# Scheduler priority for a recurrent chain, earlier K and Q copies, and a wider, doubled staging buffer

## The chip, the cores and the metric

The kernel runs on one core of a Trainium2 chip. The metric is the time on the device in microseconds. Executions of one kernel agree within about 1% here, so ratios are given with a 95% interval. A ratio is the mean time of one kernel's fast runs over that of the other's fast runs of the same rounds, so it is not quite the ratio of the medians that are quoted beside it.

## The reference, cut to what matters

```python
for s in range(n_seg):                      # 64 segments of 32 tokens
    h = concatenate([mem, x[:, 32*s:32*s+32]])   # 8 memory rows + 32 tokens, 448 wide
    q, k, v = h @ Wq, h @ Wk, h @ Wv        # 16 heads of 256
    p = softmax(mask(q k^T * scale))
    o = (p v) @ Wo
    mem = o[:, :8]                          # the next segment needs it
    outs.append(o[:, 8:])
h  = x + concatenate(outs)                  # x goes in after a layer norm
h2 = h + (silu(n(h) @ w_gate) * (n(h) @ w_up)) @ w_down
# the result, and the gradients of x, mem0 and all seven weights
```

The memory rows make 64 steps that cannot overlap, once forward and once backward.

## The kernel before

After each segment the kernel keeps K and Q, transposed as TensorE made them, and turns them token by token again for the backward stage. That side work ("spill") runs per tile of four segments, called r0 to r3 after their place in it. K's four jobs are done in r3, Q's four in the next r0; the eight memory rows of a segment are spilled likewise after each sixteenth.

```python
def _tm_quarter(stg, dst_rows, q, nrows, eng):        # one spill job
    pt = ps1(BF16)
    for j in range(8):
        c = q * 8 + j
        nc.tensor.transpose(pt[:, j * P:(j + 1) * P], stg[:, c, :], ident[:, :])
    for hq in range(2):
        tmq = work.tile([P, 512], BF16, name="tmq", bufs=1)
        k.evac(tmq[:], pt[:, hq * 512:(hq + 1) * 512], eng)   # ScalarE for K, VectorE for Q
        nc.sync.dma_start(out=dst_rows[:, ...], in_=tmq[0:nrows, :])
# per segment s, r = s % 4
ps_v = wpass(Wv_sb, s)  # ... vT, then qT and kT
# scores -> pS;  transposes of vT -> V_sb
run_deferred(4)                                        # Q's jobs (r0)
with tc.high_priority(offset=4000):
    # softmax, P_sb, transposes of P -> PT_sb
nc.vector.tensor_copy(out=qT_x[:, :, r * SEG:(r + 1) * SEG], in_=qT[:, :, 0:SEG])
nc.scalar.copy(out=kT_x[:, :, r * SEG:(r + 1) * SEG], in_=kT[:, :, 0:SEG])
if r == 3:
    tok_major_x(kT_x, ...)                             # queue K's jobs
    run_deferred(4)                                    # and do them here
# P times V -> oT, times Wo -> memory rows (VectorE) and outputs (ScalarE)
# r == 3: tok_major_x(qT_x, ...)                       # queue Q's jobs
# ... [cut: sixteenths]
```

`evac` copies a result out of the accumulators. A scheduler orders each engine's instructions from priorities and from a model of durations, so the program's order is not the built order.

## Time and profile before

5248.1 us median of 4 runs. The stages, from the trace (the end of a segment is the copy of its memory rows):

| stage | us |
|---|---|
| up to the end of the first segment | 90.9 |
| 62 further forward segments (mean 27.4) and the last | 1699.1 + 25.3 |
| drain: from there to the first feed-forward product | 103.6 |
| feed-forward, backward weights | 553.1 + 74.5 |
| first backward segment, 63 further ones (mean 25.0) | 30.2 + 1573.3 |
| weight gradients (tail) | 1089.4 |

In profile lines PE is TensorE (PEld its weight loads), ACT is ScalarE, DVE is VectorE, POOL is GpSimd and SP is SyncE; psh and psf are accumulator tiles. A line of "A <- B: total, times, longest" in the list of waits names the engine that waited and the instruction it waited for. In the view in order of time a line has start, duration, engine, line of the kernel, what was written from what, and in brackets the idle time ahead of it and who ended it. The lines themselves stand in the prediction.

### The profile page before, as it was taken

To read this page: it belongs to the slowest core of one execution; us is meant where nothing else is said; L and a number is where in the kernel's file an instruction comes from. 1 tells how busy PE (TensorE), PEld (TensorE's weight loads), DVE (VectorE), ACT (ScalarE), POOL (GpSimd) and SP (SyncE) were. 2 spreads that over 40 slices of the span, in tenths; PEclk is the share of its full clock that TensorE was granted. 3 is DMA by queue.
4 is the path that set the end of the run, shared out by engine and by line. 5 is a ranking of instruction groups with operands and counts; after the bars stand their busy time and mean duration, and the time that the engine had idled before them with its cause. 6 is when DMAs were issued, how large, how long until landed. Compare 5 with 4: busy or idle time off the path is not lost.

```text
span 5239.3 us, 201704 instructions
## 1 busy us (share of the span) xinstructions
PE 4092.1 (78%) x94192; PEld 3447.6 (66%) x94192; DVE 2149.7 (41%) x4166; ACT 1581.2 (30%) x2722; POOL 396.2 (8%) x809
## 2 busy tenths in 40 slices
PE   4777777777777737776688888888888798987849
PEld 3777777777777624333688888888888755544525
DVE  3444444444444335554333333333333344645520
ACT  2222222332232233332323222232222344342420
POOL 2000000000000100000101011011000100000100
PEclk8888888888888868898798888888888799998879
DMA  4111211111111211112523233233223333333452
GB/s 160 49 50 57 67 48 48 62 59 57 54 56 46 86 64 61 62 59 71 163 88 94 86 99 91 86 92 100 86 86 88 121 103 122 112 120 103 140 181 92
DMA packets 221334, 454.17 MB, mean 87 GB/s; under 512 B 47072, under 2 KB 126080, under 8 KB 212624
## 3 DMA queue, kind: packets, MB, share of 16 engines
q1 hardware_dynamic: 180160, 284.12, 16.9%
q0 software_dynamic: 40336, 157.14, 9.2%
q8 instruction: 737, 12.08, 1.0%
q14 instruction: 101, 0.83, 0.1%
HBM read 228.30 MB, written 208.12 MB: 83 GB/s over the span
## 4 chain that ended last, share of the span: by engine, by line
PE 48%; ACT 7%; DMA 7%; DVE 6%; issue 3%; SPq 0%; ACTq 0%; POOL 0%; DVEq 0%; POOLq 0%
PE psf L790 15%; PE psf L933 8%; ACT dO_sb L59 4%; PE psf L717 3%; PE psf L980 2%; PE psf L1014 2%; PE psf L662 2%; PE psh L894 1%; PE psf L593 1%; DMA Kx<-tmq 1%; PE psf L348 1%; PE psf L769 1%; PE psf L778 1%; PE psf L728 1%; DMA out_dram<-wres 1%
## 5 line engine op out<-in xcount | busy, mean ns | idle before, releaser
L933 PE MATMUL psf<-ktg,H_all 128*128 128x512 bf16 x1920 | 420.1, 381 | 6.6 <-ACT acc L59 6.6
L933 PEld LDWEIGHTS <-H_all 128*128 128x128 bf16 x1920 | 187.8, 98 | 233.5 <-issue 11.7
L796 DVE CAST doutT_all<-psf 128x24 bf16<-128x24 f32 x63 | 11.5, 183 | 775.5 <-PE psf L790 775.5
L790 PE MATMUL psf<-dvT,WvT_sb 128*128 128x40 bf16 x8192 | 298.0, 191 | 25.3 <-issue 24.8
L790 PE MATMUL psf<-dkT,WkT_sb 128*128 128x40 bf16 x8192 | 289.7, 189 | 15.8 <-issue 15.6
L790 PE MATMUL psf<-dqT,WqT_sb 128*128 128x40 bf16 x8192 | 283.8, 188 | 13.2 <-issue 13.1
L790 PEld LDWEIGHTS <-WvT_sb 128*128 128x128 bf16 x8192 | 271.1, 108 | 32.9 <-issue 27.4
L493 PE MATMUL psf<-oT,Wo_sb 128*128 128x40 bf16 x8192 | 271.2, 198 | 11.0 <-DVE oT L57 5.3
L790 PEld LDWEIGHTS <-WkT_sb 128*128 128x128 bf16 x8192 | 266.8, 106 | 18.2 <-issue 17.7
L493 PEld LDWEIGHTS <-Wo_sb 128*128 128x128 bf16 x8192 | 269.8, 109 | 12.8 <-issue 6.3
L790 PEld LDWEIGHTS <-WqT_sb 128*128 128x128 bf16 x8192 | 261.1, 105 | 14.8 <-issue 14.6
L59 ACT COPY dO_sb<-psh 40x1024 bf16<-40x1024 bf16 x256 | 238.4, 1006 | 100.5 <-PE psh L748 100.5
L803 ACT COPY dxnT_tile<-psf 128x96 f32<-128x96 f32 x64 | 15.2, 238 | 809.5 <-DVE doutT_all L797 797.9
L348 PE MATMUL psf<-hT_roll,Wk_sb 128*128 128x40 bf16 x8192 | 224.4, 179 | 26.2 <-issue 25.6
L894 PE MATMUL psh<-ident,kstg 128*128 128x128 bf16 x2048 | 156.7, 250 | 106.6 <-DVE kstg L886 106.6
L446 PE MATMUL psh<-ident,P_sb 40*40 40x40 bf16 x1024 | 42.5, 191 | 249.2 <-DVE P_sb L442 249.2
L348 PEld LDWEIGHTS <-Wk_sb 128*128 128x128 bf16 x8192 | 213.2, 96 | 32.1 <-issue 31.7
L940 DVE TENSOR_TENSOR acc<-acc,psf 128x512 f32<-128x512 f32 x288 | 194.8, 687 | 89.4 <-PE psf L933 88.3
L348 PE MATMUL psf<-hT_roll,Wv_sb 128*128 128x40 bf16 x8192 | 218.5, 181 | 13.9 <-DVE hT_roll L498 13.9
L348 PEld LDWEIGHTS <-Wv_sb 128*128 128x128 bf16 x8192 | 217.5, 97 | 18.1 <-issue 18.1
L717 PE MATMUL psf<-doutT_all,WoT_sb 128*128 128x40 bf16 x8192 | 218.6, 180 | 13.7 <-DVE doutT_all L796 9.0
L717 PEld LDWEIGHTS <-WoT_sb 128*128 128x128 bf16 x8192 | 217.3, 96 | 14.6 <-issue 12.6
(290 smaller groups left out, 7350.4 us busy)
## 6 DMA issues: line engine op xcount, KB each, us to landing
VT_all<-vT SPq DMA_DIRECT2D x64, 320.0 KB, 2.6
OT_all<-oT POOLq DMA_DIRECT2D x64, 320.0 KB, 2.8
vT_b<-VT_all SPq DMA_DIRECT2D x64, 320.0 KB, 3.3
dVT_all<-dvT SPq DMA_DIRECT2D x64, 320.0 KB, 2.6
dKT_all<-dkT POOLq DMA_DIRECT2D x64, 320.0 KB, 4.1
dQT_all<-dqT SPq DMA_DIRECT2D x64, 320.0 KB, 4.6
Kx<-tmq SPq DMA_DIRECT2D x128, 128.0 KB, 2.3
Qx<-tmq SPq DMA_DIRECT2D x128, 128.0 KB, 2.0
```

The lines of the kernel that those rows point to most:

```text
L59: nc.scalar.copy(out=out, in_=in_)
L348: nc.tensor.matmul(o, lhsT=W_sb[:, kc, c * P:(c + 1) * P], rhs=hT_roll[:, kc, sl, :], start=(kc == 0), stop=(kc == KC - 1))
L493: nc.tensor.matmul(pO[:, mc * L:(mc + 1) * L], lhsT=Wo_sb[:, c, mc * P:(mc + 1) * P], rhs=oT[:, c, :], start=(c == 0), stop=(c == MC - 1))
L593: nc.tensor.matmul(pg[:, 0:f1 - f0], lhsT=hnT[:, kc, :], rhs=Wg_sb[:, kc, f0:f1], start=(kc == 0), stop=(kc == KC - 1))
L662: nc.tensor.matmul(pdh[:, 0:D], lhsT=srcT[:, c, :], rhs=WT[:, c, :], start=(i == 0), stop=(i == nmm - 1))
L717: nc.tensor.matmul(o, lhsT=WoT_sb[:, kc, c * P:(c + 1) * P], rhs=doutT_all[:, kc, s, :], start=(kc == 0), stop=(kc == KC - 1))
L790: nc.tensor.matmul(pH[0:msz, mc * L:(mc + 1) * L], lhsT=WT[:, c, mcols], rhs=dT[:, c, :], start=(i == 0), stop=(i == 3 * MC - 1))
L894: nc.tensor.transpose(pt[:, j * P:(j + 1) * P], stg[:, c, :], ident[:, :])
L933: nc.tensor.matmul(pacc[:, :], lhsT=H_all[:, kt, mc * P:(mc + 1) * P], rhs=KT_sb[:, sl, ncn * 512:(ncn + 1) * 512], start=(i == 0), stop=( ...
L940: nc.vector.tensor_tensor(out=dst, in0=dst, in1=pacc[:, :], op=ALU.add)
L980: nc.tensor.matmul(pacc[:, 0:D], lhsT=KT_sb[:, sl, mc * P:(mc + 1) * P], rhs=dOut_all[:, kt, :], start=(i == 0), stop=(i == len(slots) - 1))
L1014: nc.tensor.matmul(pacc[:, 0:f1 - f0], lhsT=HN_all[:, kt, mc * P:(mc + 1) * P], rhs=X_all[:, kt, f0:f1], start=(kt == 0), stop=(kt == NT - 1))
```

## The change

Its intent is to keep the chain of dependent work ahead of everything else. The chain gets the highest priority in program order (`crit`), forward and backward; K and Q are copied out right after their projections, and the spill jobs are queued before the softmax; the spill gets a wider, doubled buffer. To make room, the input window shrinks from 12 slots to 8, qT and kT to one buffer.

```diff
+    def crit(self):                       # class _Prio; next starts at -50_000_000
+            off = self.tc.cur_priority - self.next
+            with self.tc.high_priority(offset=off):
+                yield
+                self.next = self.tc.cur_priority
-        NWIN = 12
+        NWIN = 8
-        for hq in range(2):
-            tmq = work.tile([P, 512], BF16, name="tmq", bufs=1)
-            k.evac(tmq[:], pt[:, hq * 512:(hq + 1) * 512], eng)
-            nc.sync.dma_start(out=dst_rows[:, q * 1024 + hq * 512:q * 1024 + (hq + 1) * 512], in_=tmq[0:nrows, :])
+        tmq = work.tile([P, 1024], BF16, name="tmq", bufs=2)
+        k.evac(tmq[:], pt[:, 0:1024], eng)
+        nc.sync.dma_start(out=dst_rows[:, q * 1024:(q + 1) * 1024], in_=tmq[0:nrows, :])
-    prep_tile(1)
-    prep_load(2)
+    prep_load(1)
-            prep_tile(t + 2)
+            prep_tile(t + 1)
...
+        with k.prio.crit():               # projections; likewise softmax, P times V, Wo
+            if r == 0:
+                nc.vector.tensor_copy(out=qtmp[:], in_=qT[:, :, 0:SEG])   # parked for r1
...
+            nc.scalar.copy(out=kT_x[:, :, r * SEG:(r + 1) * SEG], in_=kT[:, :, 0:SEG])
...
+        if r == 3:
+            tok_major_x(kT_x, dr["Kx"][t * P:(t + 1) * P, :], P, "s")
+            tok_major_x(qT_x, dr["Qx"][t * P:(t + 1) * P, :], P, "v")
         run_deferred(4)
-        with tc.high_priority(offset=4000):
+        with k.prio.crit():               # softmax
-        if r == 3:
-            tok_major_x(kT_x, dr["Kx"][t * P:(t + 1) * P, :], P, "s")
-            run_deferred(4)
...                                         # backward: two crit blocks round the same chain
```

## The prediction

> **What bounds the kernel now.** I first read the page's busy shares, which cover three stages with different limits: a forward recurrence of 64 segments (0 to 1815 us), a feed-forward stage, a backward recurrence of 64 segments (2550 to 4150 us) and weight gradients. The diff touches the two recurrences and the drain behind the first. Each segment needs the last one's memory rows, so a recurrence costs the sum of its segments' latencies. Next the list of who waited for whom:
>
> ```profile
> POOL P_all L449 <- DVE P_sb L442: 1328.5, 63, 26.2
> ...
> PE psh L446 <- DVE P_sb L442: 249.2, 64, 6.7
> ...
> ACT tmq L59 <- DMA Kx<-tmq: 230.3, 105, 14.8
> ...
> DVE tmq L57 <- DMA Qx<-tmq: 131.8, 71, 3.2
> ...
> POOL hn_t L580 <- DMA Km<-tmq: 85.5, 1, 85.5
> ```
>
> GpSimd's long waits cost nothing: it only issues stores. TensorE's 249 us is the softmax, 3.9 us in each of 64 segments. ScalarE and VectorE, which must also serve the chain, stand for 360 us in front of tmq, the one staging buffer through which transposed K and Q leave for memory: each copy waits until the previous store has landed. The last line is one wait of 85 us. I then read the order-of-time view of two neighbouring segments:
>
> ```profile
> 824.34 3.14 PE L358 MATMUL psh<-ident,kT_x 128*128 128x128 bf16 x32
> ...
> 827.41 1.18 PE L484 MATMUL psf<-PT_sb,V_sb 40*128 40x40 bf16 x32
> ...
> 847.78 0.59 ACT L59 COPY tmq<-psh 128x512 bf16<-128x512 bf16 x1 [3.47 <-DMA Kx<-tmq]
> 848.26 1.05 ACT L455 COPY kT_x<-kT 128x1024 bf16<-128x1024 bf16 x1
> ...
> 849.51 1.91 ACT L59 COPY V_sb<-psh 40x1024 bf16<-40x1024 bf16 x2
> 850.71 0.42 DVE L57 COPY tmq<-psh 128x512 bf16<-128x512 bf16 x1 [2.47 <-ACT V_sb L59]
> 851.32 0.74 ACT L436 ACTIVATE S_sb<-S_sb 40x640 f32<-40x640 f32 x1
> ```
>
> The reader sees the K transposes stand between the P transposes and P times V, and in the next segment a spill copy that waits for a store push the V copies and the exponential back by about 3 us. From the same view I took phase means, leaving out the first tile; segments are named by place in a tile of four (r0 to r3). r2, where no spill runs, is the clean one:
> - whole segment: r0 28.7, r1 27.8, r2 24.5, r3 27.6 us; the three after each sixteenth, with the extra memory-row spills, 28.3, 28.4, 29.3.
> - scores to exponential: 7.3, 7.0, 4.4, 4.8; P transposes to P times V: 1.2, 1.3, 1.2, 4.0; waiting for the first projection: 0.9, then 0.05.
>
> So the excess over r2 (4.2, 3.3, 0, 3.1) is all of the kind that the change addresses. Behind the last segment:
>
> ```profile
> 1815.00:1938.00 123.00, 38.08 (x332) 27.80 (x329) 34.82 (x113) 37.71 (x66) 11.56 (x78) 0.60 0.30 93
> ```
> ```profile
> 1832.99 0.58 ACT L59 COPY tmq<-psh 128x512 bf16<-128x512 bf16 x1 [14.85 <-DMA Kx<-tmq]
> ...
> 1907.75 0.58 ACT L59 COPY tmq<-psh 128x512 bf16<-128x512 bf16 x1 [1.98 <-DMA Km<-tmq]
> ...
> 1910.56 0.16 POOL L580 MEMSET hn_t<- 128x64 bf16 x1 [85.48 <-DMA Km<-tmq]
> ```
>
> From 1815 to 1938 us every compute engine is idle two thirds of the time. The feed-forward buffers lie where the forward pools were, so they wait for the last of some 28 staged stores, 2.45 us each, after a first stall of 15 us behind the weight loads.
>
> The backward recurrence is different: TensorE is busy 88% there, its orders are nearly final, and only the first segment of each tile is longer (26.05 us against 24.2 to 24.9).
>
> [...] at 847.78 the ready V copies stand 3.47 us behind a copy that waits for a store. [...] 128 KB stores land in 2.0 to 2.3 us, 256 KB ones (gradient results) in 2.4. So one store of twice the size costs little more than one of the small.
>
> **The change part by part.** I compared the built order of the changed kernel with the old one.
>
> 1. Staging: 128x1024 copies instead of pairs of 128x512, in two buffers instead of one. A copy costs 1.0 us on ScalarE and 0.7 on VectorE (the 40x1024 and 128x1024 copies of this trace) against 2 x 0.58 and 2 x 0.42. Per job the chain copy, store, copy, store of about 5 us becomes half of 1.0 + 2.4: about 1.6 us. So four jobs fit into one segment and no longer spill into the next.
>
> 2. Order: the chain has its own top priority, and Q and K are copied out right after their projections. In the new order the K transposes (r3) stand before the P transposes, under the softmax; three of four input transposes move there in r0. The clean r2 keeps its order except for trivial swaps: 24.5 stays.
> - r1: no staging is left in it: 27.8 becomes 24.6, saving 3.2.
> - r3: P transposes to P times V falls by 2.75, but one ScalarE copy of 1.0 us now stands before the exponential (+0.7 against its old 4.8) and two later ones wait for a store, delaying the attention output by perhaps 0.2: 25.8, saving 1.8.
> - r0: input transposes save 0.3 before the first projection; the exponential comes at 4.9, not 7.3 (an input copy of 0.59 stands before it); VectorE has two Q copies and the move of the parked first quarter of Q (0.43) inside the softmax, +0.3; output copies +0.3: 26.4, saving 2.3.
> - after a sixteenth: 26.4, 25.0, 26.1, saving 1.9, 3.4, 3.2.
> Sum: 12 x 2.3 + 12 x 3.2 + 15 x 1.8 + 3 x (1.9 + 3.4 + 3.2) = 27.6 + 38.4 + 27 + 25.5 = 118 us.
>
> 3. Drain: K leaves within the last segment; 12 wide jobs stay. Two stores queue behind the weight loads (17 us, as now), then 10 jobs at 1.7 us, plus some waiting for the transposed feed-forward weights that the new order mixes in, about 7: the buffers are free 41 us after the chain instead of 95. I take 52 off, as weight transposes may hold the first tile.
>
> 4. Backward: the layer-norm work (3.9 us of VectorE, an input copy) moves from the head of a tile, where doT waits for it, to the time under the long last product:
> ```profile
> 2750.17 0.66 PE L811 MATMUL psf<-identf,dxnT_tile 128*128 128x128 f32 x4 [0.66 <-ACT dxnT_tile L803]
> ...
> 2755.54 0.37 PE L728 MATMUL psf<-vT_b,doT 128*40 128x40 bf16 x8 [0.52 <-DVE doT L57]
> ```
> Three of the four transposes go too. Of the excess of about 1.4 us I take 1.1, 15 times: 16 us.
>
> 5. Start: one input tile is prepared before the first projection, not three: 3 us. The smaller window (8 slots) and the single qT and kT buffers are free of waits, as their readers finish within the segment.
>
> Total 118 + 52 + 16 + 3 = 189; 5248 - 189 = 5059, say 5060 us, 3.6% less.
>
> **The rivals.**
> - The staging wait returns in a new place: ScalarE's third and fourth K copies stand before its share of the attention output. [...] Against: by the times above the fourth ends 5.1 us after the exponential begins, when the output is just ready. If 256 KB stores took 3.5 us, r3 would lose 1.1 and r0 0.5 more, some 25 us: 5085.
> - Copying K and Q early stretches the softmax and eats the gain: for it, VectorE's 1.8 us of inserted copies; against, 0.74 us of them lie beside the exponential. If all were exposed, 1 us in each of 20 segments: 5080.
> - The drain is bounded by weight loading and transposing, not by staging: loads end 18 us after the chain, 170 transposes with their copies took 21 us. Then about 20 of the 52 us are lost: 5080.
> - A denser TensorE is throttled: its granted clock is already 0.84 to 0.85 in the forward stage at 77% busy, but 0.85 to 0.88 in the backward one at 88%. So I expect no drop; one of 2% in the forward products would cost about 20 us.
> - Stall by stall the new order could be better than I think, and r0 and r3 come to 25: 5025.
>
> **Range and chances.** No rival alone undoes the gain; two together give 5110 to 5125. Low end: full drain gain and near-clean segments, 5005. More than 2% faster means under 5145, a gain of 103 us, just over half of what I add up; each of the two large terms would have to fail. I give that 0.07, and 0.01 to slower.
>
> **What would show each step.** Right: waits for tmq stores on ScalarE and VectorE fall from 230 and 132 us to under 100 together; r1 as long as r2; P transposes to P times V about 1.3 us everywhere; the forward stage ends near 1695 us, and the first feed-forward product comes about 70 us after it, not 122; the backward stage takes about 1557 us, not 1573. Wrong: r2 growing, a new ScalarE wait before the attention output over 1 us, or a long wait of the feed-forward stage for weights.

The 2.4 us of a wide store are the landing time of the 256 KB result stores in the trace of before. That a copy always waits its turn on its engine was the premise; the trace shows it at 847.78 us.

## The result, and the profile after

5032.2 us median (5006.8 to 5055.9, 10 runs) against 5239.9 us (16 runs): ratio 0.9602, 95% interval 0.9581 to 0.9622. The predicted 5060 us was 28 us too high, and the range holds the result. The stages of the two traces, in us:

| | start | 62 fwd | last | drain | feed-fwd | to bwd | first bwd | 63 bwd | tail | sum |
|---|---|---|---|---|---|---|---|---|---|---|
| before | 90.9 | 1699.1 | 25.3 | 103.6 | 553.1 | 74.5 | 30.2 | 1573.3 | 1089.4 | 5239.3 |
| after | 83.1 | 1563.9 | 25.2 | 47.0 | 553.3 | 73.8 | 31.6 | 1584.0 | 1077.0 | 5038.8 |
| change | -7.8 | -135.2 | -0.1 | -56.6 | +0.2 | -0.7 | +1.4 | +10.7 | -12.4 | -200.5 |

The list of waits of the changed kernel has these lines left on tmq:

```profile
POOL hn_t L606 <- DMA Km<-tmq: 29.8, 1, 29.8
...
ACT tmq L77 <- DMA Kx<-tmq: 24.9, 32, 1.1
...
DVE tmq L75 <- DMA Qx<-tmq: 17.5, 4, 15.0
```

ScalarE and VectorE now wait 42 us for stores instead of 362 in the two lines shown before. The longest wait on ScalarE is 1.1 us, and VectorE's 17.5 us are nearly all one wait in the drain. In order of time, an r3 and the next r0 of the changed kernel:

```profile
853.37 1.96 PE L376 MATMUL psh<-ident,kT_x 128*128 128x128 bf16 x32
...
854.83 1.01 ACT L77 COPY tmq<-psh 128x1024 bf16<-128x1024 bf16 x1
855.74 0.74 ACT L494 ACTIVATE S_sb<-S_sb 40x640 f32<-40x640 f32 x1
...
858.66 0.72 PE L504 MATMUL psh<-ident,P_sb 40*40 40x40 bf16 x16 [3.33 <-DVE P_sb L500]
...
859.96 1.22 PE L514 MATMUL psf<-PT_sb,V_sb 40*128 40x40 bf16 x32 [0.57 <-DVE PT_sb L75]
860.47 1.01 ACT L77 COPY tmq<-psh 128x1024 bf16<-128x1024 bf16 x1 [1.07 <-DMA Kx<-tmq]
...
861.26 4.36 PE L524 MATMUL psf<-oT,Wo_sb 128*128 128x40 bf16 x128
...
880.46 1.27 DVE L75 COPY tmq<-psh 128x1024 bf16<-128x1024 bf16 x2
880.86 0.74 ACT L494 ACTIVATE S_sb<-S_sb 40x640 f32<-40x640 f32 x1
```

The K transposes lie under the softmax, P times V follows the P transposes without them, and in r0 no copy stands ahead of the exponential waiting for a store. The fourth spill copy does wait 1.07 us on ScalarE, right in front of that engine's share of the attention output (861.38). It costs the chain nothing: the product with Wo starts at 861.26 on what VectorE has copied and runs through. Behind the last segment, which ends at 1672.2 us:

```profile
1690.07 0.69 DVE L75 COPY tmq<-psh 128x1024 bf16<-128x1024 bf16 x1 [15.01 <-DMA Qx<-tmq]
...
1707.01 1.93 ACT L77 COPY tmq<-psh 128x1024 bf16<-128x1024 bf16 x2 [0.85 <-DMA Km<-tmq]
...
1711.46 0.16 POOL L606 MEMSET hn_t<- 128x64 bf16 x1 [29.77 <-DMA Km<-tmq]
...
1719.12 3.17 PE L619 MATMUL psf<-Wg_sb,hnT 128*128 128x512 bf16 x7 [0.68 <-ACT hnT L77]
```

The feed-forward buffers are free 39 us after the chain's end. The same product before, which tells the old drain:

```profile
1918.92 5.68 PE L593 MATMUL psf<-Wg_sb,hnT 128*128 128x512 bf16 x16 [0.68 <-ACT hnT L59]
```

That is 104 us after the old chain's end at 1815.3. The two recurrences as a whole, before and then after; columns are the stretch, its length, busy time of TensorE, weight loads, VectorE, ScalarE, GpSimd, then the granted clock (the share of full speed that the profile's clock records give TensorE), the DMA share and GB/s:

```profile
91.00:1790.00 1699.00, 1302.19 (x39952) 1262.43 (x39952) 762.24 (x1492) 495.84 (x853) 80.61 (x158) 0.84 0.17 55
2577.00:4150.00 1573.00, 1393.23 (x43395) 1343.38 (x43391) 530.08 (x1080) 454.98 (x786) 150.15 (x292) 0.87 0.30 90
```
```profile
83.00:1647.00 1564.00, 1247.26 (x39957) 1210.96 (x39957) 768.11 (x1441) 489.31 (x784) 81.37 (x160) 0.87 0.17 60
2378.00:3962.00 1584.00, 1410.99 (x43402) 1358.23 (x43398) 534.05 (x1080) 452.65 (x787) 150.13 (x292) 0.85 0.30 89
```

Forward, TensorE's idle time falls from 397 to 317 us, and its busy time by 55 us although the instructions are nearly the same in number. Backward, the idle time falls from 180 to 173 us, and yet the stage is 11 us longer because the same products take 18 us more at a lower clock. Two questions come from this: which part of the change did the forward stage's work, and is the backward part worth anything?

### The profile page after: what moved, and what is told of

Read it like the earlier page. It is cut to its first block, busy times and chain, and to the rows that moved or that the text cites. A ratio compares the mean times of both kernels' runs of the same rounds, so it can differ in the third digit from the quotient of the medians.

```text
span 5038.8 us, 201072 instructions
## 1 busy us (share of the span) xinstructions
PE 4039.7 (80%) x94192; PEld 3398.0 (67%) x94192; DVE 2156.9 (43%) x4102; ACT 1565.8 (31%) x2642; POOL 396.4 (8%) x809
## 5 line engine op out<-in xcount | busy, mean ns | idle before, releaser
L818 PE MATMUL psf<-dqT,WqT_sb 128*128 128x40 bf16 x8192 | 290.2, 189 | 31.9 <-issue 31.6
L366 PEld LDWEIGHTS <-Wk_sb 128*128 128x128 bf16 x8192 | 212.7, 96 | 25.6 <-issue 25.3
```

What stands on the lines that cost most here:

```text
L366: nc.tensor.matmul(o, lhsT=W_sb[:, kc, c * P:(c + 1) * P], rhs=hT_roll[:, kc, sl, :], start=(kc == 0), stop=(kc == KC - 1))
L818: nc.tensor.matmul(pH[0:msz, mc * L:(mc + 1) * L], lhsT=WT[:, c, mcols], rhs=dT[:, c, :], start=(i == 0), stop=(i == 3 * MC - 1))
```

## The experiments

Twelve kernels ran, in three groups of four, each group on another chip with its own runs of the kernel before; so compare ratios, not times, between groups. All results were correct. The table has the ratio to before, and from each profile the forward stage (62 segments), the drain and the backward stage (63 segments), in us.

| run | ratio | 95% interval | fwd | drain | bwd |
|---|---|---|---|---|---|
| before | 1 | | 1699 | 104 | 1573 |
| changed | 0.9602 | 0.9581 to 0.9622 | 1564 | 47 | 1584 |
| e1 staging alone | 0.9682 | 0.9637 to 0.9726 | 1572 | 49 | 1573 |
| e2 order alone | 0.9831 | 0.9790 to 0.9872 | 1615 | 97 | 1573 |
| e3 no forward priority | 0.9582 | 0.9543 to 0.9620 | 1551 | 46 | 1542 |
| e4 two small buffers | 0.9771 | 0.9734 to 0.9808 | 1596 | 62 | 1582 |
| e5 one wide buffer | 0.9797 | 0.9776 to 0.9819 | 1599 | 73 | 1594 |
| e6 no backward priority | 0.9658 | 0.9629 to 0.9687 | 1560 | 48 | 1604 |
| e7 weights behind | 0.9642 | 0.9622 to 0.9662 | 1560 | 45 | 1593 |
| e8 filled gap | 0.9610 | 0.9589 to 0.9632 | 1544 | 46 | 1566 |
| e9 changed again | 0.9631 | 0.9606 to 0.9657 | 1560 | 47 | 1574 |
| e10 no priority, filled | 0.9615 | 0.9589 to 0.9642 | 1545 | 47 | 1572 |
| e11 backward priority alone | 0.9989 | 0.9963 to 1.0014 | 1677 | 100 | 1569 |
| e12 window alone | 1.0000 | 0.9972 to 1.0029 | 1692 | 102 | 1587 |

Theory 1 was that the wait for staged stores is the larger part; theory 2, that the new order of the chain is.

### e1: staging alone

```diff
 # on the kernel before
-        for hq in range(2):
-            tmq = work.tile([P, 512], ..., bufs=1)    # copy and store, twice
+        tmq = work.tile([P, 1024], BF16, name="tmq", bufs=2)
+        ...                                            # copy and store, once
-        kT = work.tile([P, MC, L], BF16, name="kT")
+        kT = work.tile([P, MC, L], BF16, name="kT", bufs=1)
```

> The kernel before with only the staging of the change: copies of 128x1024 in two buffers (kT is cut to one buffer to make room). Theory 1, the staging wait is the larger part: spills no longer reach r1, r0 loses its wait before the softmax, r3 keeps its K transposes between P transposes and P times V (2.75 us). Forward stage about 92 us shorter (r0 26.2, r1 24.6, r3 27.2 us), drain 54 us shorter, together about -145 us, 5095 us. Theory 2, the new order of the chain is the larger part: only the drain gains, -60 us, 5180 us.

5052.5 us against 5230.2 us: 178 us of the change's 208 come from the buffer (with kT cut to one, which no run tests by itself), more than theory 1 had. The longest lines on tmq stores in its list of waits are:

```profile
POOL hn_t L579 <- DMA Km<-tmq: 31.6, 1, 31.6
...
DVE tmq L57 <- DMA Qx<-tmq: 18.3, 2, 16.6
```

ScalarE's copies into tmq wait 4 us for stores in all, and VectorE's hardly outside the drain. Segment means (over all segments of a place) are r0 25.9, r1 24.7, r2 24.4, r3 26.6 us, against 28.6, 28.0, 25.5, 27.6 before. P transposes to P times V is still 4.1 us in r3: that is what is left for the new order to gain. Theory 2 is out for this part.

### e2: order alone

```diff
 # on the changed kernel
-        tmq = work.tile([P, 1024], BF16, name="tmq", bufs=2)
+        for hq in range(2):
+            tmq = work.tile([P, 512], BF16, name="tmq", bufs=1)   # as before
```

> The changed kernel with the old staging (128x512 in one buffer). Theory 1: r3 gains the 2.75 us of the K transposes but the wait for stores stays in r0 and r1 and in the drain: forward -30 us, drain within 10 us of before, start -8: about -40 us, 5200 us. Theory 2: most of the 207 us remains, at least -130 us, 5110 us.

5129.9 us, 100 us less than before, where theory 1 had 40 and theory 2 at least 130. The waits are nearly all there, and so is the drain of 97 us:

```profile
ACT tmq L77 <- DMA Kx<-tmq: 154.6, 88, 10.7
...
DVE tmq L75 <- DMA Qx<-tmq: 125.5, 69, 3.7
...
POOL hn_t L607 <- DMA Km<-tmq: 79.7, 1, 79.7
```

The forward stage gains 84 us. r3 is 24.9 us and r0 26.3, but r1 stays at 27.7: spill copies still reach into it, with 7.0 us from the scores to the exponential, as before. So the parts are not additive. Alone they save 178 and 100 us (the second with everything of the change but the buffer), together 208: much of what the order removes in r3 and r0 is time in which copies wait for stores, and the wider buffer has removed that already.

### e3: no forward priority

```diff
 # on the changed kernel, forward stage
-        with k.prio.crit():
+        with contextlib.nullcontext():        # softmax: tc.high_priority(offset=4000), as before
```

> The changed kernel with the forward chain's own priority taken out again (the softmax gets its old raised priority back); earlier copies, queueing of jobs and staging stay. Its built order differs from the changed kernel's in three input transposes and in one V copy against the row maximum. If the place of the copies in the program does the work: within 15 us of the changed kernel, 5030 to 5050 us, r0 longer by about 0.3 to 0.6 us because of the input transposes, r1 to r3 the same. If the priority does it: over 60 us slower than the changed kernel.

5006.7 us, 0.9582 of before. That is below the range, but its interval overlaps the changed kernel's (0.9602), so what is shown is that the forward priority gives no gain that can be seen. The phase from the scores to the exponential is 0.1 to 0.4 us shorter without it in r0 and r1 (4.36 and 4.31 against 4.74 and 4.45), where priority in program order puts both of VectorE's V copies ahead of the row maximum. r0 as a whole is no shorter (25.7 us in both): without priority the input transposes cost it 0.25 us before the first projection, and the stretch from the exponential to the P transposes 0.27 us. P times V follows the P transposes after 1.2 us here too, and after 4.1 us in e1, e11 and e12. By exclusion, then, what moved the K transposes is the place of the copies and of the queueing in the program; no run has that alone.

### e4 and e5: two small buffers, one wide buffer

```diff
 # e4, on the kernel before
-            tmq = work.tile([P, 512], BF16, name="tmq", bufs=1)
+            tmq = work.tile([P, 512], BF16, name="tmq", bufs=2)
 # e5, on the kernel before: one copy and store of 128x1024, bufs=1
```

> The kernel before with two staging buffers of the old 128x512 size. If overlap of copy and store is what counts, a job takes two times half of 0.6 + 2.4 us, 3 us instead of 5: drain about 35 us shorter, forward about 55, together -90 us, 5150 us. If only the number of stores (their fixed time) counts: under -30 us.

> The kernel before with copies and stores of 128x1024, but still one buffer: copy and store cannot overlap, there are half as many stores. A job is 1.0 + 2.4 = 3.4 us, against 5 before and 1.6 to 1.7 with two wide buffers. If time per job is what counts: drain 104 - 10 x 1.6 = 88 us, forward about 80 us shorter, together about -95 us (5135 us), less than the -128 us of two small buffers. If the number of stores counts and overlap little: near the -178 us of both.

e4 saves 128 us (5102.6 against 5230.2) and e5 108 us (5123.5 against 5231.5); both changes save 178. So neither width nor doubling is enough alone. e4 was better than the 90 us expected; e5 lies a little over its 95 us, with a drain of 73 us instead of 88. Time per job counts, as the order by drain shows: 104, 73 (one wide), 62 (two small), 49 us (two wide). A wide store (256 KB) lands in 2.4 us in the median of the changed kernel's page, a small one (128 KB) in 2.0 to 2.3 us before; stores of results in the trace of before took 1.7 us with 64, 112 and 128 KB and 2.4 us with 256 KB. So twice the size added 0.1 to 0.7 us here, and most of a store's time did not grow with it.

### e6, e9 and e11: the backward priority

```diff
 # e6, on the changed kernel: backward chain as in the kernel before
-        with k.prio.crit():
 # e11, on the kernel before: only the backward chain's crit blocks
+        with k.prio.crit():
 # e9: the changed kernel, unedited
```

> The changed kernel with the backward stage of the kernel before (no priority there). If the change's backward part is real: TensorE's idle time in the backward stage goes back from 160 to 173 us to about 180 us, the first segment of a tile from 25.0 to 26.2 us, and the kernel is 5 to 20 us slower than the changed one (ratio to before 0.962 to 0.965). If it does nothing: idle time 165 to 173 us, the first segment 25 us, same time.

> The changed kernel itself, unedited, on this chip, so that the next three stand beside it. Ratio to before 0.957 to 0.963. Its second trace shows how much of a stage's time is chance: forward within 10 us of 1564, TensorE idle in the backward stage again 160 to 175 us, while the backward stage's length follows its half-clock time (10.4 us shorter than without priority at the same half-clock time, 0.43 us per us of it).

> The kernel before with only the backward priority of the change. Backward idle time of TensorE falls from 180 to 160 to 173 us, the first segment of a tile from 26.2 to 25.0 us, the stage by about 10 us at the same half-clock time; kernel 0.997 to 0.999 of before, so perhaps not told apart from 1. If the part is nothing: idle time stays at 180.

By time the part cannot be told from nothing: e11 is 0.9989 with 1 inside its interval, and e6's 0.9658 overlaps e7's 0.9642, which stood beside it with the priority. The backward stage varies from 1542 to 1604 us across traces. The trace tells more. The clock records give only full and half clock (217 of each in the trace of before, 202 of each in that of the changed kernel), so each stage has a half-clock time. In six traces without the backward priority (before, e1, e4, e5, e6, e12) TensorE is idle 178 to 192 us in the stage, mean 183; in eight with it (changed, e2, e3, e7 to e11) 159 to 174, mean 167. A line fitted to the fourteen stage lengths over half-clock time has a slope of 0.38 us per us and puts those with the priority 11 us lower, with single traces up to 9 us off it. The longest place, the first segment of a tile, falls from 26.4 to 25.1 us in the mean. In the changed kernel its head looks like this:

```profile
2556.36 3.36 PE L744 MATMUL psf<-doutT_all,WoT_sb 128*128 128x40 bf16 x128
...
2559.64 1.03 PE L755 MATMUL psf<-vT_b,doT 128*40 128x40 bf16 x32
...
2562.70 0.44 PE L839 MATMUL psf<-identf,dxnT_tile 128*128 128x128 f32 x2
```

The product with doT no longer waits, and the input-gradient transposes run between later products. So the part does what it should, and by that line the changed kernel's +10.7 us in that stage is the clock: 461 us at half clock in its profile, 416 in that of before. The priority itself does not bring this: the mean half-clock time is 438 us with it and 444 without.

### e7: weights behind

```diff
 # on the changed kernel
-    nc.sync.dma_start(out=Wd_sb[:], in_=...)
+    nc.gpsimd.dma_start(out=Wd_sb[:], in_=...)     # after Wg and Wu; transposed last
```

> The changed kernel with the third feed-forward weight loaded behind the other two by GpSimd, not by SyncE ahead of the Q stores (its transposes are done last). If the 15 us wait of VectorE before the third Q copy of the drain comes from the queue order behind that load: the wait falls below 6 us, and the drain from 47 to about 38 us, kernel -9 us. If the transfer engines are simply full with the weights: wait and drain stay, within 3 us.

```profile
POOL hn_t L606 <- ACT WdT_sb L77: 26.1, 1, 26.1
...
DVE tmq L75 <- DMA Qx<-tmq: 13.4, 4, 6.6
```

The long wait fell from 15.0 to 6.6 us, but the drain only from 47.0 to 45.0 us, not to 38. Over half of that wait was queue order, and it was nearly free: with it gone, the feed-forward buffers wait for the last transposed weight (the first line) instead of the last store. This run is bound by the weights, their transposes and the layer norm behind them. It also loads and transposes the third weight last, so what would bound the changed kernel's own drain next is not shown.

### e8 and e10: filling the softmax gap

The forward stage's busy time fell by 55 us, and the granted clock rose from 0.84 to 0.87. The clock records last 3.4 us or whole multiples of it (all but one of the 434 before and of the 404 after). Before the change 51 idle gaps of TensorE in the forward stage are longer than 3.4 us and 81 drops to half clock occur; after it 28 and 63. That such gaps bring the drops was the guess, and two kernels that filled the softmax gap tried it.

```diff
 # e8, on the changed kernel, after the V transposes
+            if r in (1, 2):
+                pw = ps1(BF16)
+            for j in range(48 if r in (1, 2) else 0):
+                nc.tensor.transpose(pw[:, ...], ident[:, :], ident[:, :])    # never read
 # e10, on e3, after run_deferred(4), in all segments
+        for j in range(32 if deferred else 48):    # counted before run_deferred
+            nc.tensor.transpose(pw[0:L, ...], vT[:, j % 32, :], ident[:, :])
```

> The changed kernel with 48 transposes of the identity, whose result nobody reads, on TensorE between the V transposes and the P transposes of r1 and r2 only (r0 and r3 have such work there already). If idle gaps of TensorE cost it clock afterwards: the half-clock time of r1 and r2 falls from about 14% to 7 to 10% of the segment, and each is 0.8 to 1.5 us shorter, 25 to 50 us for the kernel (5000 us), r0 and r3 as before. If the clock is held down by load: half-clock time the same or more, r1 and r2 the same or longer.

> The changed kernel without the forward chain's priority and with transposes that nobody reads filling what is left of the softmax gap in every segment (48, or 32 where spill transposes stand there). If the half clock after idle gaps costs 0.2 to 0.4 us per us: forward half-clock time falls from 400 to under 250 us, the forward stage from 1564 (changed) or 1551 (without priority) to about 1515 us, the kernel to about 4980 to 5000 us, 0.7% or more below the changed kernel beside it. If the fill collides with the chain or the clock does not matter there: no gain over the changed kernel.

In e8 the half-clock time of r1 and r2 fell by more than half (7.5 and 7.2 to 3.0 and 3.3 us), r0 and r3 kept theirs. (The expectation's 14% counts lost clock: 7.5 us at half clock are 30% of r1, and 15% lost.) Against the changed kernel the segments gained 0.9 and 0.3 us, at the edge of what was expected and below it, and the kernel's 0.9610 overlaps e7's 0.9642 beside it. e10 took the forward half-clock time from 403 (e9) to 260 us, yet the stage was 15 us shorter than in e9 beside it and 6 us shorter than in e3, not 36 to 49, and the kernel's 0.9615 lies inside the interval of e9's 0.9631. The expectation failed. The end of a segment of e10 in order of time, and then a product with Wo of e9, tell why:

```profile
800.48 2.84 PE L486 MATMUL psh<-ident,vT 128*40 128x128 bf16 x48
804.88 0.57 PE L509 MATMUL psh<-ident,P_sb 40*40 40x40 bf16 x16 [1.55 <-DVE P_sb L505]
806.02 1.17 PE L519 MATMUL psf<-PT_sb,V_sb 40*128 40x40 bf16 x32 [0.57 <-DVE PT_sb L76]
807.27 3.96 PE L529 MATMUL psf<-oT,Wo_sb 128*128 128x40 bf16 x128
811.51 3.35 PE L367 MATMUL psf<-hT_roll,Wv_sb 128*128 128x40 bf16 x128 [0.28 <-DVE hT_roll L534]
```
```profile
889.81 4.43 PE L524 MATMUL psf<-oT,Wo_sb 128*128 128x40 bf16 x128
```

The fill stands there, the gap is 1.55 us, and the product with Wo still takes 3.96 us where a full-clock pass of the same shape (the last line of the first fence) takes 3.35: in the clock records the drop comes at 806.2 us, in P times V, and lasts until 809.6. Over the stage, 198 of its 259 us are at half clock in e10, against 236 of 267 in e9; the three projections run at full clock but for at most 14 us, save in e4 and e5 (56 and 41 us). One gap over 3.4 us is left in e10 and still 62 drops occur, 48 of them during P times V or the product with Wo; in e9 10 of 63 come there, and 32 in the softmax gap. So the fill mostly took half-clock time out of the gap and the transposes, where it cost little, and moved the drops to the short products behind it. It was not the wrong kind of work: 60 stretches of 3.4 us at full clock in e10 held only transposes, over 60% busy, and full clock followed each of them. The price is small besides: the pass of e9 lies wholly in a half-clock record (888.6 to 895.4 us), and 4.43 against 3.35 us is 1.1 us for a whole pass. Over 128 products that is 26 ns each at full clock and 35 ns at half, 1.3 times as long, not twice.

What cost 55 us of busy time before was not in the projections or in Wo (881 us of busy time before, 880 after, summed over the four): it was the rest, 421 against 367 us, with 212 and 100 us at half clock. Nearly all of it is transposes: those of V fell from 149 to 124 us, and those of K from 52 to 29, where the 32 of a tile took 3.14 us behind the P transposes before and take 1.96 us ahead of them now.

### e12: window alone

```diff
 # on the kernel before
-        NWIN = 12
+        NWIN = 8
-    prep_tile(1)
-    prep_load(2)
+    prep_load(1)
 # and one tile ahead instead of two in the loop
```

> The kernel before with only the smaller window (8 slots) and one tile prepared ahead. The first segment ends at 83 to 87 us instead of 91 to 94, the forward segments are as before, kernel -5 to -8 us (0.9985 to 0.999). If the single preparation is too late for the chain: longer r0.

The first segment ends at 86.1 us instead of 90.9. The kernel's time cannot be told from before (1.0000, 0.9972 to 1.0029), as an effect of this size could not. r0 (29.0 against 28.7 us) does not wait longer for prepared input: the first projection starts 0.94 us into it, against 0.90. So the window mainly makes room. How much is needed is not shown: two wide buffers did not fit beside the 12 slots and doubled kT (e1 without its cut of kT does not build: a pool wants 34.5 KB per partition where 33.0 are left), but e1 fits them by cutting kT alone.

No version here beats the changed kernel beyond the intervals: e3 (0.9582), e8 (0.9610) and e10 (0.9615) lie among its two ratios, 0.9602 and 0.9631, or within 0.2% of them.

## Why the prediction was right

The mechanisms of its two large terms, forward and drain, held. That the total came so near is in part luck: in the stages of the two traces, 201 us against 189, backward missed by 27 us one way, and forward, drain, start and the untouched tail together by 39 us the other.

- **Forward segments: -118 predicted, -135 measured** (-139 in e9's trace). By place, without the tiles after a sixteenth: r0 25.65 us (26.4 predicted), r1 24.60 (24.6), r2 24.51 (24.5), r3 25.47 (25.8); after a sixteenth 25.8, 25.2, 24.6 (26.4, 25.0, 26.1). r1 equals r2, and P transposes to P times V is 1.2 to 1.3 us everywhere, as announced. In sum r0 was mis-sized most, by 0.75 us: its output copies, put at 0.3 us, cost the chain nothing (P times V to Wo 1.29 us, as in r2), the copies inside the softmax, put at 0.3 us, added nothing either (3.02 us from the exponential to the P transposes before and after), and its exponential comes at 4.74 us, not 4.9. Its listed terms also add up to 2.1 us, not to 2.3.
- **Which part did it:** the prediction credited staging and order together. e1 and e2 show that staging alone gives -127 us forward and order alone -84, so that they overlap, and e3 that the priority is not needed.
- **Drain: -52 predicted, -57 measured.** Buffers free 41 us after the chain was predicted, 39 measured. The two landmarks that it announced were misread: the first feed-forward product came 104 us after the chain before, not 122, and comes after 47, not 70. The saving was derived from the buffers, so it held. e1 (49) and e2 (97) show that it is the staging alone.
- **Backward: -16 predicted; +10.7 in the profile.** The step that failed is the announced stage length of 1557 us: the trace had 1584, and 1574 in e9. The idle time fell by 16 us in the mean of the traces, and the length by 11 us at equal half-clock time. The mechanism was right, and the sum left out that this stage's clock varies by more than the effect.
- **Start: -3 predicted, -7.8 measured**, -4.8 in e12 and -4.2 in e9. The first projection starts at 53.3 us in the changed kernel's profile, at 59.8 before: 6.5 us for the two tiles, not 3. The mean end of the first segment is 85.6 us in the nine traces with the small window and 92.1 in the five without.
- **Rivals.** ScalarE's wait ahead of the attention output came, at 1.07 us just over the 1 us that was named as a sign of being wrong, and cost the chain nothing: that sign looked at a wait off the chain. The softmax did stretch, 4.74 us in r0 and 5.20 in r3 against 4.50 in r2 from scores to exponential, within the sum. The feared lower clock did not come forward, where it rose from 0.84 to 0.87. The weights bound the drain only in e7, after the staging had given what it had. Any two of the four rivals with losses add up to 5100 to 5105 us, not to 5110 to 5125.
- **Left open:** the tail, whose instructions the change does not touch, was 12 us shorter in the profile and 1074 to 1081 us in six of the seven traces of changed versions with both order and backward priority, against 1082 to 1090 us in the others. It follows the clock: a line through the fourteen tails has a slope of 0.31 us per us at half clock and leaves none over 3.4 us off, with 240 us at half clock before and 212 after. Why that time differs, no run tells.

## What to carry to other kernels

Where an engine serves both a dependent chain and side work, look first at the side work's buffer. Here a copy that waited 3.47 us for its predecessor's store (at 847.78 us, before the change) held up the V copies behind it, which were ready, and another buffer with a larger store took a few lines and gave 178 of 208 us. Do not add the gains of two remedies that remove the same wait. When a stage's length varies with the clock, as the backward stage did here (1542 to 1604 us), judge a small part by idle time and by its own waits across several traces, not by one total.

## What the traces show of the clock and of stores beside other traffic

- **The clock:** gaps of over 3.4 us were not needed for a drop. The backward stage before the change has a longest idle gap of 2.8 us and 73 drops to half clock; TensorE was busy 63% of the mean 3.4 us ahead of a drop, mostly with products of 40 rows. In e10 one gap over 3.4 us was left in the forward stage and 62 drops occurred. The busy share tells more. In the two recurrences of the fourteen traces, cut into 3.4 us as the clock records are: of 728 stretches at full clock that were busy under 40%, all were followed by half clock; of 5227 busy 90% or more, 5 were; between them it was mixed. In the traces of before and of the changed kernel alone it was 118 of 118, 1 of 717, and between them 179 of 511.
- **Stores:** a 256 KB store landed in 2.4 us in the median of the changed kernel. Its four of Q in the drain, beside 4.7 MB of weight loads and with one of these ahead in their own queue, took 9.3 us in the median. In e7, with none ahead, the longest wait of VectorE for one of them was 6.6 us, against 15.0.
